# Order of the relu sums, halved GpSimd scaling and the weight of a batch's last values in a fused attention and channel-MLP kernel

## The chip, the cores and the metric

The kernel runs on one core of one Trainium2 chip. The metric is the device time of one execution in microseconds (us). It is given as the median of several executions.

Engine names are short: PE multiplies matrices (PEld is its weight load, which runs beside it), DVE is VectorE, ACT is ScalarE, POOL is GpSimd, and SP issues most DMAs.

## What is computed

For 8 batches of 12 heads, 448 rows and a head width of 64, attention runs on root-mean-square normalised q and k. Its output, laid out as `x` with 768 columns, then goes through a low-rank mix along the rows and a channel MLP with a hidden width of 3072:

```
q_n, k_n = rmsnorm(q, g_q), rmsnorm(k, g_k)
attn = softmax(q_n @ k_n.T / 8);  x = attn @ v          # 8 x 448 x 768
h = x.T @ U @ V                                         # rank 32, along the rows
u = x + h.T
out = u + relu(u @ w_ch1) @ w_ch2                       # 768 -> 3072 -> 768
```

## The kernel before

**Attention.** Work goes by pairs of heads: pair p holds two heads of batch p // 6, so a batch has six pairs. For a pair, squares (`squares`, on ACT for the later pairs) are summed on DVE (`reduce`, L233), ACT turns the sums into factors (`rsqrt`, L238 and L239), and `scale` (L244) multiplies q and k by them. From pair 12 on, `scale` is one GpSimd instruction over 112 x 1024 elements, and SP transposes its result by DMA (`dma_transposes`, L277). `scores` (L295) makes the four 112-column blocks of the scores. Every third block goes into two single banks of PSUM (named `sh` in the profile, drawn from the four-bank pool `mm`), and the others go into a pool of their own (`sc`). ACT takes the exponentials (`expo`, L303). `values` then multiplies by v into a bank of `mm` (`products`, L310), and DVE divides by the row sums and writes `x` (`normalize`, L325 to L338). Its last instruction, L338, is the last reader of that bank.

**MLP.** Tiles of 128 rows are taken two at a time (`mlp_pair`, twelve of them). In its first half, 24 hidden blocks are computed two by two: 12 matmuls (L523) fill a bank `ph`, and a relu (L527; the instruction is L420 on ACT or L422 on DVE) empties it into four quarters of `hT`, called A11, A21, A12 and A22. The second half is Strassen's product in Winograd's form: seven products of 12 matmuls (L511) instead of eight. It needs three sums of relu's output, S1 = A21 + A22, S2 = S1 - A11 and S3 = A11 - A21 (L532 to L534), which DVE makes for four blocks at a time, and a fourth, S4 = A12 - S2 (L556), in three instructions after the third product. S3 is written over A21 and S4 over A12. All of them read two bf16 operands from SBUF. In the first such pair, `combine` (L507) also still makes sums of the weights. The product banks, like `ph`, `o` and `sh`, come from the four-bank pool `mm`.

**What sets the order.** The program is emitted by hand into in-order queues, one for each engine. The MLP is a generator that yields after every step (6 or 12 matmuls). Each yield hands control back to `weave` (L678), which has a list of attention pieces with weights and spreads them over a stretch of the MLP: before each piece it takes MLP steps (`step`, L672) until the piece's share of the columns is done. In `attention`, the last two pieces of a batch are its pair 5's two `values` (L666, L667), with weight 1 each. The sums of relu's output are emitted inside the MLP step that also emits the relu, so they stand on DVE ahead of whatever attention piece follows that step. After batch 7, a plain loop runs the rest of the MLP (L913).

Of the kernel before, what the change touches and what calls it, by code (L numbers as in the profile page):

```python
# [14 lines left out]
OP = AluOpType  # L15
# [3 lines left out]
def kernel(  # L19
# [13 lines left out]
    nc = tc.nc  # L33
    B, H, S, D = q.shape
# [6 lines left out]
    NJ = 4  # L41
    SP = S // NJ
# [72 lines left out]
    def rs_of(p, n=1, of=None):  # L115

        c = 16 * (p % 6)
        return (of or (banks0[3][0:SP] if p < 8 else rms))[:, c:c + 16 * n]
# [122 lines left out]
    def scale(p):  # L241
        t, a = divmod(p, 2)
        qkns[p] = norm.tile([SP, NJ, 4, D], BF16, tag="qkn", name="qkn", bufs=2)
        (nc.gpsimd if p >= 12 else nc.vector).tensor_tensor(  # L244
            qkns[p].rearrange("p j g d -> p g j d"),
            qk_of[t][0:SP, a].rearrange("p s h (j d) -> p (s h) j d", d=D),
            rs_of(p).rearrange("p (g j) -> p g j ()", j=NJ).to_broadcast([SP, 4, NJ, D]),
            OP.mult)

    def k_side(p):  # L250

# [250 lines left out]
    S3, S4 = A21, A12  # L502
# [6 lines left out]
    def product(bank, left, right, start, cols=slice(0, HALF)):  # L509
        for k in range(KH // 2):  # L510
            nc.tensor.matmul(bank, left[:, k, :], right[:, k, cols], start=start and k == 0,  # L511
                             stop=k == KH // 2 - 1, skip_group_check=not start)
            if k == 5:
                yield cols.stop - cols.start

    def mlp_pair(g):
        t0, u, last = 2 * g + 2, u_of(2 * g + 2, 2), 2 * g + 4 == 28
        for k in range(KH // 2):
            ph = ps_mm.tile([P, 4, P], FP32, tag="mm", name="ph")
            for j in range(2):  # L520
                hc, out = 2 * k + j, ph[:, 2 * j:2 * j + 2].rearrange("p a n -> p (a n)")
                for dc in range(KD):
                    nc.tensor.matmul(out, w1b[:, dc, hc * P:(hc + 1) * P], u[:, dc, :],  # L523
                                     start=(dc == 0), stop=(dc == KD - 1))
                if j == 0:
                    yield 2 * P
            relu(hB[:, 0:4, k, :], ph, k % 3)  # L527
            if g == 1 and k in (1, 4, 7, 9):
                combine(12 + (1, 4, 7, 9).index(k))
            if k % 4 == 3:  # L530
                ks = slice(k - 3, k + 1)
                nc.vector.tensor_tensor(S1[:, ks], A21[:, ks], A22[:, ks], OP.add)  # L532
                nc.vector.tensor_tensor(S2[:, ks], S1[:, ks], A11[:, ks], OP.subtract)  # L533
                nc.vector.tensor_tensor(S3[:, ks], A11[:, ks], A21[:, ks], OP.subtract)  # L534
            yield 2 * P
        have_read([t0, t0 + 1])
        x0, x1 = x_of(t0), x_of(t0 + 1)
        c0, c1 = slice(0, HALF), slice(HALF, dm)
        osb0, osb1 = new_osb(), new_osb()

        def bank():
            return ps_mm.tile([P, HALF], FP32, tag="mm", name="po")

        W = bank()
        yield from product(W, A11, B11, True)
        nc.scalar.copy(part, W)
        yield HALF
        Z = bank()
        yield from product(Z, A22, T4, True)
        nc.vector.tensor_tensor(osb1[:, c0], Z, x1[:, c0], OP.add)  # L550
        yield HALF
        yield from product(W, A12, B21, False)
        nc.vector.tensor_tensor(osb0[:, c0], W, x0[:, c0], OP.add)
        for k in range(0, KH // 2, 4):
            ks = slice(k, k + 4)
            nc.vector.tensor_tensor(S4[:, ks], A12[:, ks], S2[:, ks], OP.subtract)  # L556
        if last:
            put(t0, osb0, c0)
        yield HALF
        X = bank()  # L560
        yield from product(X, S2, T2, True)
        nc.vector.tensor_tensor(osb0[:, c1], X, part, OP.add)  # L562
        nc.gpsimd.tensor_tensor(osb0[:, c1], osb0[:, c1], x0[:, c1], OP.add)  # L563
        yield HALF
        parts = [slice(0, HALF // 2), slice(HALF // 2, HALF)] if last else [slice(0, HALF)]
        Ys = [bank() for _ in parts]
        for Y, c in zip(Ys, parts):
            d = slice(HALF + c.start, HALF + c.stop)
            yield from product(Y[:, c], S1, T1, True, c)
            nc.vector.tensor_tensor(osb1[:, d], Y[:, c], x1[:, d], OP.add)  # L570
            yield c.stop - c.start
        yield from product(X, S3, T3, False)
        nc.vector.tensor_tensor(part, X, part, OP.add)  # L573
        both = osb1.rearrange("p (h n) -> p h n", h=2)
        nc.gpsimd.tensor_tensor(both, both, part.rearrange("p n -> p () n").to_broadcast([P, 2, HALF]), OP.add)  # L575
        put(t0 + 1, osb1)
        yield HALF
        for Y, c in zip(Ys, parts):
            d = slice(HALF + c.start, HALF + c.stop)
            yield from product(Y[:, c], S4, B22, False, c)  # L580
            nc.vector.tensor_tensor(osb0[:, d], Y[:, c], osb0[:, d], OP.add)
            if last:
                put(t0, osb0, d, (nc.sync, nc.scalar))
            yield c.stop - c.start
        if not last:
            put(t0, osb0)

    def attention(b):
        items = []

        def add(weight, fn, *args):
            items.append((weight, lambda: fn(*args)))

        starts = (0, 3, 6, 8, 11, 14, 16, 19, 22) if b == 1 else range(0, 24, 3)
        ends = dict(zip(starts, [*starts[1:], 24]))
        apart.update((6 * b + i // 4, i % 4) for i, e in ends.items() if e - i == 3)

        def run(p, kc):
            i = 4 * (p - 6 * b) + kc
            if i in ends:  # L600
                add(3 if i == 3 else 2 if b == 1 and i % 8 == 0 or b == 2 and i == 0 else 1, session, i)
            add(0 if i in ends else 1, expo, p, kc)

        def session(i):
            for j in range(i, ends[i]):
                scores(6 * b + j // 4, (j % 4,))

        for p in range(b * 6, b * 6 + 6):
            t, odd = divmod(p, 2)
            early = p < 12  # L610
            if p == 12:
                add(0, gains, p)
            run(p, 0)
            if p == 11:
                add(0, touch, 7)
                add(0, load, 7)
                add(0, load_v, 7)
            elif p >= 13 and p + 3 < NP:
                add(0, reduce, p + 3)
            elif early and odd:  # L620
                add(0, rsqrt, p + 1, 2)
                add(0, scale, p + 1)
            elif early and p > 6:
                add(0, scale, p + 1)
            run(p, 1)
            if not odd and p >= 14 and p + 2 < NP:
                add(0, rsqrt, p + 2, 2)
            if p >= 12 and p + 2 < NP:
                add(0, scale, p + 2)
                add(0, dma_transposes, p + 2)  # L630
            if p % 6:
                add(1, values, p - 1, 0)
            if p == 11:
                add(0, reduce, 12)
            if early and not odd:
                add(0.5, transposes, p + 1)
                if p < 10:
                    add(0, reduce, p + 2)
            if p + 1 < NP and p > 11:
                add(0, gains, p + 1)  # L640
            run(p, 2)
            if p % 6:
                add(1, values, p - 1, 1)
            if early and not odd:
                if p < 10:
                    add(0, reduce, p + 3)
                for a in range(2):
                    if p != 8:
                        add(0, squares, (10 if p == 6 else 12) + a)
            if p >= 12 and t + 2 < NT:  # L650
                add(0, squares, p + 4, "act")
            if odd and p > 11:
                if t + 3 < NT:
                    add(0, load, t + 3)
                if t + 2 < NT:
                    add(0, load_v, t + 2)
            if not odd and t + 1 < NT:
                add(0, cast_v, t + 1)
            run(p, 3)
            if early and odd and p < 11:  # L660
                add(1, transposes, p + 1)
            if p == 9:
                add(0, touch, 6)
                add(0, load, 6)
                add(0, load_v, 6)
        add(1, values, b * 6 + 5, 0)  # L666
        add(1, values, b * 6 + 5, 1)  # L667
        return items

    at = [0.0]  # L670

    def step(fill):  # L672
        n = next(fill, None)
        if n is not None:
            at[0] += n
        return n
# [170 lines left out]
    with tc.manual_schedule():  # L847
# [62 lines left out]
        for b, key in ends.items():  # L910
            weave(fill, place(key, 0.05), attention(b))
            weave(fill, place(key, 0.6), mixing(b))
        for _ in fill:  # L913
            pass


# [28 lines left out]
```

## Time and profile before

| what | value |
|---|---|
| median of 3 runs | 573.9 us (572.37 to 574.25) |
| profiled execution, its own time | 574.8 us |
| its span in the profile | 572.9 us |
| PE busy | 557.1 us, 97% |
| DVE busy | 349.2 us, 61% |
| ACT busy | 305.1 us, 53% |
| POOL busy | 169.5 us, 30% |
| mean share of the TensorE clock granted | 0.997 |

The span runs from the first to the last recorded instruction, and the execution's own time is 1.9 us longer. A row of the waits view reads: engine and line that waited, then the engine and line that ended the wait, then us in total, number of waits and the longest. A row of the timeline reads: start, duration, engine, line, operation, output and input tiles, shapes, count, and in brackets the idle time before it with what ended it. Waits of PE are counted from the modelled end of the matmul before, those of PEld from the end of the last weight load.

### The profile page before, as it was taken

To read this page: it belongs to the slowest core of one execution; us is meant where nothing else is said; L and a number is where in the kernel's file an instruction comes from. 1 tells how busy PE (TensorE), PEld (TensorE's weight loads), DVE (VectorE), ACT (ScalarE), POOL (GpSimd) and SP (SyncE) were. 2 spreads that over 40 slices of the span, in tenths; PEclk is the share of its full clock that TensorE was granted. 3 is DMA by queue.
4 is the path that set the end of the run, shared out by engine and by line. 5 is a ranking of instruction groups with operands and counts; after the bars stand their busy time and mean duration, and the time that the engine had idled before them with its cause. 6 is when DMAs were issued, how large, how long until landed. Compare 5 with 4: busy or idle time off the path is not lost.

```text
span 572.9 us, 13177 instructions
## 1 busy us (share of the span) xinstructions
PE 557.1 (97%) x5468; PEld 389.2 (68%) x5469; DVE 349.2 (61%) x766; ACT 305.1 (53%) x515; POOL 169.5 (30%) x139
## 2 busy tenths in 40 slices
PE   7999999999999999989999999999999999999996
PEld 3665665767677587676785775776867758777784
DVE  5967867687655655665566678376565554643332
ACT  6966540779267563586547770765716745202020
POOL 5956025343052230531313430432304320010101
PEclk9999999999999999998999999999999999999999
DMA  8999996955373561554447564635606101040101
GB/s 272 279 243 237 204 264 167 203 146 160 99 129 115 137 156 43 123 148 128 94 132 157 138 159 89 148 85 154 163 15 135 31 17 57 9 103 2 56 1 56
DMA packets 108284, 72.39 MB, mean 126 GB/s; under 512 B 56656, under 2 KB 104768, under 8 KB 108224
## 3 DMA queue, kind: packets, MB, share of 16 engines
q1 hardware_dynamic: 96704, 61.70, 42.3%
q0 software_dynamic: 11008, 9.44, 10.2%
q8 instruction: 43, 0.70, 0.5%
q10 hardware_dynamic: 512, 0.41, 0.2%
q14 instruction: 17, 0.14, 0.1%
HBM read 56.78 MB, written 11.01 MB: 118 GB/s over the span
## 4 chain that ended last, share of the span: by engine, by line
PE 80%; DVE 9%; DMA 4%; ACT 2%; POOL 1%; issue 1%; SPq 1%; POOLq 0%; DVEq 0%; ACTq 0%
PE ph L523 32%; PE po L511 25%; PE o L310 6%; PE sc L295 4%; PE ph L448 3%; PE po L466 3%; PE sh L295 3%; DMA qkT<-qkn 2%; DVE hT L534 2%; DVE xr L389 1%; DMA hT<-in_q_dram 1%; DVE hT L532 1%; ACT hT L420 1%; DVE hT L533 1%; DVE comb L507 1%
## 5 line engine op out<-in xcount | busy, mean ns | idle before, releaser
L523 PE MATMUL ph<-ur,w1b 128*128 128x256 bf16 x1728 | 204.2, 274 | 1.3 <-DVE xr L338 1.3
L523 PEld LDWEIGHTS <-w1b 128*128 128x128 bf16 x1728 | 164.9, 98 | 32.0 <-issue 9.6
L511 PEld LDWEIGHTS <-hT 128*128 128x128 bf16 x1032 | 96.3, 98 | 66.4 <-issue 9.7
L420 ACT ACTIVATE hT<-ph 128x512 bf16<-128x512 f32 (+1 forms) x112 | 65.9, 589 | 110.7 <-PE ph L523 103.3
L303 ACT ACTIVATE E<-sc 112x896 bf16<-112x896 f32 x138 | 123.1, 918 | 2.4 <-PE sc L295 2.3
L244 POOL TENSOR_TENSOR qkn<-qk,rms 112x1024 bf16<-112x1024 f32 x36 | 70.5, 1959 | 124.1 <-ACT rms L239 99.0
L511 PE MATMUL po<-w2b,hT 128*128 128x384 bf16 (+1 forms) x588 | 104.4, 323 | 0.2 <-ACT hT L420 0.2
L303 ACT ACTIVATE E<-sh 112x448 bf16<-112x448 f32 x108 | 53.4, 543 | 90.3 <-PE sh L295 90.3
L511 PE MATMUL po<-comb,hT 128*128 128x384 bf16 (+1 forms) x444 | 78.8, 322 | 0.4
L422 DVE TENSOR_SCALAR hT<-ph 128x512 bf16<-128x512 f32 (+1 forms) x58 | 38.6, 666 | 51.3 <-PE ph L523 47.7
L563 POOL TENSOR_TENSOR osb<-osb,xr 128x384 f32<-128x384 f32 x12 | 11.0, 913 | 191.4 <-DVE osb L562 185.4
L310 PEld LDWEIGHTS <-E 112*128 112x128 bf16 x1536 | 61.1, 98 | 9.3 <-issue 1.6
L310 PE MATMUL o<-va,E 112*128 112x65 bf16 x1344 | 57.2, 194 | 0.6 <-ACT E L303 0.5
L532 DVE TENSOR_TENSOR hT<-hT 128x512 bf16<-128x512 bf16 x36 | 21.0, 583 | 34.8 <-ACT hT L420 33.6
L233 DVE TENSOR_REDUCE sums<-sq 112x16 f32<-112x1024 f32 x32 | 38.7, 1210 | 3.8 <-ACT sq L228 3.8
L295 PE MATMUL sc<-qkT 64*128 64x448 bf16 x268 | 39.9, 351 | 0.7 <-ACT qkT L282 0.3
L325 DVE RECIPROCAL rec<-o 128x4 f32<-128x4 f32 x84 | 15.0, 178 | 40.3 <-PE o L310 39.7
L466 PE MATMUL po<-w2b,hT 128*128 128x384 bf16 x192 | 35.2, 326 | 0.1
L295 PEld LDWEIGHTS <-qkT 64*128 64x128 bf16 x376 | 14.9, 94 | 28.9 <-issue 14.6
L228 ACT ACTIVATE sq<-qk 112x1024 f32<-112x1024 f32 x32 | 33.7, 1054 | 0.0
L334 DVE TENSOR_TENSOR xr<-o,rec 128x192 bf16<-128x192 f32 (+1 forms) x108 | 31.5, 310 | 2.9
L575 POOL TENSOR_TENSOR osb<-osb,part 128x768 f32<-128x768 f32 x12 | 21.8, 1813 | 37.1 <-DVE part L573 37.1
(123 smaller groups left out, 520.5 us busy)
## 6 DMA issues: line engine op xcount, KB each, us to landing
qk<-in_q_dram SPq DMA_DIRECT2D x44, 256.0 KB, 4.2
qk<-in_k_dram SPq DMA_DIRECT2D x44, 256.0 KB, 4.8
vt<-in_v_dram SPq DMA_DIRECT2D x17, 512.0 KB, 5.9
w1b<-in_moe_w_ch_dram POOLq DMA_DIRECT2D x6, 768.0 KB, 21.6
w2b<-in_moe_w_ch_dram POOLq DMA_DIRECT2D x6, 768.0 KB, 34.0
out_dram<-osb SPq DMA_DIRECT2D x8, 336.0 KB, 3.0
comb<-in_v_dram SPq DMA_DIRECT2D x5, 512.0 KB, 8.7
out_dram<-osb SPq DMA_DIRECT2D x7, 288.0 KB, 3.0
```

The source lines that it names most:

```text
L228: nc.scalar.activation(dst, src, AF.Square)
L233: nc.vector.tensor_reduce(rs_of(p, of=sums).rearrange("p (s h j) -> p s h j", s=2, h=2)[:, :, hs], sqs[p].rearrange("p (s h j d) -> p s h ...
L244: (nc.gpsimd if p >= 12 else nc.vector).tensor_tensor(qkns[p].rearrange("p j g d -> p g j d"), qk_of[t][0:SP, a].rearrange("p s h (j d) -> ...
L295: nc.tensor.matmul(sc[hh][0:n, 0:S], flat[pp, c:c + n], blocks(p)[pp, :, 0], start=True, stop=True)
L303: nc.scalar.activation(dst, src, AF.Exp, scale=float(D) ** 0.5)
L310: nc.tensor.matmul(o[:, i, :], E[:, hh, c:c + P], va[:, hl, kc, :], start=(kc == 0), stop=(kc == NJ - 1))
L334: nc.vector.tensor_tensor(xr[:, k:k + n, d0:d0 + D], o[:, i:i + n, 0:D], rec[:, i:i + n].rearrange("p c -> p c ()").to_broadcast([P, n, D] ...
L420: nc.scalar.activation(out, ph, AF.Relu)
L422: nc.vector.tensor_relu(out, ph)
L466: nc.tensor.matmul(po, left(hc), w2b[:, half, hc, :], start=(hc == 0), stop=(hc == KH - 1))
L511: nc.tensor.matmul(bank, left[:, k, :], right[:, k, cols], start=start and k == 0, stop=k == KH // 2 - 1, skip_group_check=not start)
L523: nc.tensor.matmul(out, w1b[:, dc, hc * P:(hc + 1) * P], u[:, dc, :], start=(dc == 0), stop=(dc == KD - 1))
```

## The change

It has four edits:

1. `scale` on GpSimd (pairs 12 to 47) is issued as two instructions of 112 x 512 elements, one for q's half of the heads and one for k's, in place of one of 112 x 1024. For the pairs scaled on DVE nothing is different.
2. The sums S1, S2, S3 and S4 of every MLP pair, and four of the `combine` sums, are not emitted where they stood. They are put in a list `pending`, and each call of `step` first emits the oldest one of the list, then the MLP step. So at most one sum precedes each MLP step, and the attention pieces that `weave` puts between the step with the relu and the next one come ahead of it.
3. The first of a batch's last two `values` gets weight 2 in place of 1, so that one more share of the MLP stands between it and the piece before it.
4. The last loop calls `step`, so that it too empties the list.

```diff
@@ scale @@
-        (nc.gpsimd if p >= 12 else nc.vector).tensor_tensor(
-            qkns[p].rearrange("p j g d -> p g j d"),
-            qk_of[t][0:SP, a].rearrange("p s h (j d) -> p (s h) j d", d=D),
-            rs_of(p).rearrange("p (g j) -> p g j ()", j=NJ).to_broadcast([SP, 4, NJ, D]),
-            OP.mult)
+        out = qkns[p].rearrange("p j g d -> p g j d")
+        x = qk_of[t][0:SP, a].rearrange("p s h (j d) -> p (s h) j d", d=D)
+        rs = rs_of(p).rearrange("p (g j) -> p g j ()", j=NJ)
+        for g in (slice(0, 2), slice(2, 4)) if p >= 12 else (slice(0, 4),):
+            (nc.gpsimd if p >= 12 else nc.vector).tensor_tensor(
+                out[:, g], x[:, g], rs[:, g].to_broadcast([SP, g.stop - g.start, NJ, D]), OP.mult)
@@ mlp_pair @@
+    pending = []
+
+    def later(fn, *args):
+        pending.append(lambda: fn(*args))
+
...
-                combine(12 + (1, 4, 7, 9).index(k))
+                later(combine, 12 + (1, 4, 7, 9).index(k))
             if k % 4 == 3:
                 ks = slice(k - 3, k + 1)
-                nc.vector.tensor_tensor(S1[:, ks], A21[:, ks], A22[:, ks], OP.add)
-                nc.vector.tensor_tensor(S2[:, ks], S1[:, ks], A11[:, ks], OP.subtract)
-                nc.vector.tensor_tensor(S3[:, ks], A11[:, ks], A21[:, ks], OP.subtract)
+                later(nc.vector.tensor_tensor, S1[:, ks], A21[:, ks], A22[:, ks], OP.add)
+                later(nc.vector.tensor_tensor, S2[:, ks], S1[:, ks], A11[:, ks], OP.subtract)
+                later(nc.vector.tensor_tensor, S3[:, ks], A11[:, ks], A21[:, ks], OP.subtract)
...
-            nc.vector.tensor_tensor(S4[:, ks], A12[:, ks], S2[:, ks], OP.subtract)
+            later(nc.vector.tensor_tensor, S4[:, ks], A12[:, ks], S2[:, ks], OP.subtract)
@@ attention @@
-        add(1, values, b * 6 + 5, 0)
+        add(2, values, b * 6 + 5, 0)
         add(1, values, b * 6 + 5, 1)
@@ step @@
     def step(fill):
+        if pending:
+            pending.pop(0)()
         n = next(fill, None)
...
-        for _ in fill:
+        while step(fill) is not None:
             pass
```

## The prediction

> **What bounds the kernel now.** I read the page first, then the waits, then the timeline around the longest wait, then one table of stages and a few rows of durations.
>
> ```profile
> PE 557.1 (97%) x5468; PEld 389.2 (68%) x5469; DVE 349.2 (61%) x766; ACT 305.1 (53%) x515; POOL 169.5 (30%) x139
> PE 80%; DVE 9%; DMA 4%; ACT 2%; POOL 1%; issue 1%; SPq 1%; POOLq 0%; DVEq 0%; ACTq 0%
> ```
>
> PE is the bound: it is idle for only 572.9 - 557.1 = 15.8 us. About 5 us of that is the tail after the last matmul, some 3.5 us more is in the first 40 us (PE is busy for 16.74 and 19.73 us of the first two 20 us), and neither is touched by the change. What can be won is therefore single microseconds: PE's gaps between about 120 and 500 us. The chain puts 9% on DVE, about 50 us, but most of that ran while PE multiplied; it is no measure of a gain. The waits name the gaps.
>
> ```profile
> DVE hT L532 <- ACT hT L420: 33.6, 22, 3.2
> ...
> PEld L295 <- DVE xr L338: 4.8, 7, 1.9
> ...
> PE sh L295 <- DVE xr L338: 3.5, 6, 1.6
> ...
> PEld L523 <- DVE xr L338: 2.0, 2, 1.1
> ...
> PE ph L523 <- DVE xr L338: 1.3, 2, 0.6
> ...
> PE o L310 <- ACT E L303: 0.5, 1, 0.5
> ```
>
> The largest waits of PE on an engine end at L338, the last reader of an `o` bank: PE wants a bank of `mm` and normalize has not emptied it. Why it is late is seen in the timeline of the longest such wait:
>
> ```profile
> 253.56 0.47 DVE L532 TENSOR_TENSOR hT<-hT 128x512 bf16<-128x512 bf16 x1 [1.16 <-ACT hT L420]
> 253.70 1.23 POOL L214 CAST va<-vt 112x1024 bf16<-112x1024 f32 x1
> ...
> 254.07 1.14 DVE L533 TENSOR_TENSOR hT<-hT 128x512 bf16<-128x512 bf16 x1
> ...
> 254.90 2.07 POOL L244 TENSOR_TENSOR qkn<-qk,rms 112x1024 bf16<-112x1024 f32 x1
> 255.13 2.12 DVE L534 TENSOR_TENSOR hT<-hT 128x512 bf16<-128x512 bf16 x1
> ...
> 257.17 0.17 DVE L325 RECIPROCAL rec<-o 128x4 f32<-128x4 f32 x1
> ...
> 257.91 0.36 PE L295 MATMUL sh<-qkT 64*128 64x448 bf16 x1 [1.59 <-DVE xr L338]
> ```
>
> A sum that starts under a running GpSimd instruction lasts until just after that one ends: L534 from 255.13 to 257.25, L244 to 256.97. Alone it takes 0.42 us. So three sums of 1.2 us become 3.7 us, they stand ahead of normalize, and PE stands for 1.59 us. The rows of durations say the same (min/median/max in ns):
>
> ```profile
> L534 DVE TENSOR_TENSOR hT<-hT x36: 415/418/2123, 132.3 to 555.7; 128x512 bf16<-128x512 bf16 x36
> L244 POOL TENSOR_TENSOR qkn<-qk,rms x36: 1898/1905/2409, 92.5 to 456.8; 112x1024 bf16<-112x1024 f32 x36
> ```
>
> The same picture (sums stretched to 1.1 to 2.1 us, then a late normalize) stands before the waits near 188, 307, 332, 386 and 460 us. Near 125 us it is `combine` that is stretched. The wait near 257 us has a second cost. The table of stages has length, busy times of PE, PEld, DVE, ACT and POOL, and the granted clock:
>
> ```profile
> 255.30:258.70 3.40, 1.81 (x14) 0.82 (x13) 3.37 (x6) 2.10 (x4) 1.67 (x1) 1.00 0.40 77
> 258.70:262.10 3.40, 3.40 (x18) 2.41 (x17) 0.88 (x1) 1.79 (x4) 0.00 (x0) 0.50 0.92 236
> ```
>
> After the one stretch in which PE was busy for only 1.81 of 3.40 us, the clock is 0.50 for 3.40 us, and half of those, 1.7 us, is lost.
>
> **The change part by part.**
>
> *Sums one per step, behind the attention pieces* (edit 2). It removes no instruction. Where three sums stood ahead of a normalize, there is now none, or one or two that were left from steps before. It acts on the nine waits for L338. PE's rows give 3.5 + 1.3 = 4.8 us; PEld's give 4.8 + 2.0 = 6.8 us. At 257 us the two `sh` matmuls start 1.94 us apart (255.97 and 257.91), though elsewhere in the trace the two start together; PEld's 1.85 is the nearer to that, so I take 6.8 us, with 4.8 as the other end. With the 1.59 us stand gone the halved clock should go: 1.7 us, or nothing if other gaps fall into one such stretch.
>
> The sums also leave a blocking place: L532 stood 33.6 us in 22 waits for ACT's relu, with normalize queued behind it. A step later that relu is mostly done. What is late next: S2 is read by the fourth product, S4 by the last. The last S1, S2, S3 are out by the third step after the last relu, and the fourth product starts with the seventh; a step of 6 matmuls takes 0.98 us (chain rows "PE po L511 x6"), so three steps or more, 3 us, cover a sum of 0.42 to 2.1 us. The S4 sums have as many. I cost these new waits at nothing; without that cover they are a rival below.
>
> *GpSimd scaling in halves* (edit 1). It adds 36 instructions. A blocked sum now waits at most for one half, about 1905 / 2 = 0.95 us, in place of 1.9. That DVE does get in between two GpSimd instructions is in the trace: at 183.28 us a sum waits out one L244, runs, and the cast issued after it lasts 1.24 in place of 1.04 us. The fixed cost of a GpSimd instruction has two bounds. L575 takes 1813 ns for twice the elements of L563 at 913 ns: 2 x 913 - 1813 = 13 ns. L778 takes 402 ns for 128 columns and 834 for 384: 1.69 ns a column, so 186 ns fixed. I take 13 to 186, near the first, as those are of the longer kind. POOL is 30% busy, which hides it, except where the chain runs through a scaling and its transpose (97.89 and 107.52 us, pairs 12 and 13): two times 0.01 to 0.19, I take 0.2 us in all.
>
> Before a sum that meets a half there is a residue: in five of the nine places one sum of about 0.42 us may still stand ahead of a normalize, half of the time under a half. I take 0.3 us each, 1.5 us in all; 0 and 5 x 0.95 = 4.8 are the ends.
>
> *More MLP ahead of the last values* (edit 3). The wait of L310 for an exponential, 0.5 us near 146 us, is at a batch's last values and should go. All earlier pieces of a batch move forward by a few per cent of a stretch, by a step at most. Those are six matmuls each way, covered by a PE queue that is full; I take nothing, with 0.5 us either way per batch as bounds (the longest wait of that kind), some 3 us.
>
> *The last loop* (edit 4) has no attention beside it: nothing.
>
> **The sum.** Against the profiled execution: 574.8 - 6.8 - 1.7 + 1.5 + 0.2 - 0.5 = **567.5 us**. That execution is 0.9 us above the median of 573.9, and the runs spread by 1.9 us, about one halved stretch of clock. From the median it would be 566.6 if that run had it, 568.3 if not; I keep 567.5.
>
> **The Trainium skill, two places.** The trace halves the clock after 1.59 us of standing in 3.4 us. The page "TensorE: Matmul & The Clock Gate", section "Why this matters for your kernels", advises against gaps over some 3 us, which would make this stretch no consequence of the gap: by it the sum would be 569.2. The row above it decides here. And the rows bound a GpSimd instruction's fixed cost by 13 and 186 ns, while the page "GPSIMD Engine Reference", section "3.1 Elementwise — side-by-side cycle accounting", has about 156 ns for DVE's dispatch and two hops in place of one on GpSimd, which speaks against halving; by that, an estimate of 0.3 us a scaling, the two places in the chain would cost 0.6, a sum of 567.9.
>
> **The rivals.**
>
> - *The sums stay in the way.* One per step is still one ahead of each normalize, and each meets a half. For it: the largest stretch of scaling (two L244 and a cast, 5 us) is longer than two steps. Against it: one blocked sum is 1.3 us, not 3.7. Then only half of 6.8 goes, with the clock: 574.8 - 3.4 - 1.7 + 0.2 = 569.9, or 571.6 without the clock. About 571.
> - *The gain is given back.* PE goes faster into ACT, busy 17.19 of the 20 us from 125 to 145. PE's gaps would then end at the exponentials. Against it: over the span ACT is 53% busy and its waits for PE (103.3 us at L420) show slack. Time 573 to 575.
> - *Slower: a product waits for its sum.* S2 or S4 is pushed behind attention work and halves of scaling until the fourth or the last product has to stand. It decides once DVE is more than three steps, 3 us, behind. Price: about 1 us in each of the nine pairs beside attention. With the gain of the first part reduced to 4.8 and the clock lost again: 574.8 - 4.8 + 1.5 + 9 = 580.5; with half the pairs, 576. Against it: the longest stretched run of sums was 3.7 us and DVE is 61% busy.
>
> **How the numbers follow.** Forecast 0.62 (own range 565 to 570), sums in the way 0.15, given back 0.11, slower 0.12. The low end, 564.0, has no residue and also ends 2 us of the smaller waits (L295 for ACT's L282, 1.5; L361 for L338, 0.6). The high end, 573.4, takes in the second case and the edge of the third. What a measurement of this kernel tells from no change is about 0.3%, 1.7 us. Faster by more: 0.62 + 0.15 less a little, 0.76; within: 0.12; slower: 0.12.
>
> **What would show it.** Right: the waits of PE and PEld for L338 fall below 2 us together, no sum lasts over 1.4 us, the clock is 1.00 from 125 to 510 us, and PE's idle falls by some 6 us. Half instructions of L244 near 960 to 1,050 ns. Wrong: waits of L511 for DVE's sums, new waits of L310 for L303, or a stretch of half clock at another place.

## The result and the profile after

The changed kernel takes **566.64 us** (median of 6 runs, 566.12 to 568.81), the kernel before 573.83 us in the same job (6 runs, 572.37 to 576.21). The ratio is 0.988, with a 95% interval from 0.9854 to 0.9907. The forecast was 567.5. The profiled execution of the changed kernel took 566.27 us, with a span of 564.5, against 574.8 and 572.9.

Its page, with busy times and shares of the span first and the chain by engine after it:

```profile
PE 552.0 (98%) x5469; PEld 388.2 (69%) x5469; DVE 339.7 (60%) x766; ACT 303.8 (54%) x515; POOL 179.3 (32%) x175
...
PE 89%; ACT 4%; DVE 2%; DMA 2%; issue 1%; SPq 0%; POOLq 0%
```

PE is idle for 12.5 us in place of 15.8, and the chain's share of DVE falls from 9% to 2%. DVE's busy time falls by 9.5 us though it does the same work: S1 to S4 take 7.9 us less (76.3 to 68.4) and the `combine` sums 2.1 less; other rows are up by some 0.5. That is time in which a sum waited for GpSimd and was counted as busy. The middle of the kernel, in one table of stages (length, then PE, PEld, DVE, ACT and POOL busy, then the clock), once for the kernel before and once for the changed one, each up to its eleventh MLP pair's start:

```profile
125.00:509.00 384.00, 377.82 (x3711) 269.03 (x3712) 235.15 (x534) 215.82 (x357) 100.76 (x66) 1.00 0.44 109
```

```profile
125.00:500.00 375.00, 373.39 (x3714) 268.09 (x3713) 226.92 (x532) 214.54 (x357) 109.87 (x97) 1.00 0.44 112
```

All that was won, 9 us in these two executions, lies here. PE's idle time in the stage falls from 6.2 to 1.6 us. The other 4.4 us are in its busy time. The stretch of half clock is 1.7 of them. Another 1.7 are `sh` matmuls (17.4 to 15.7 us in the stage): two that start together take 0.36 us of PE, and two that start apart 0.36 each. What the rest is stays open. The waits of the changed kernel (L339 is L338 of before, L296 is L295, L304 is L303, L529 is L523):

```profile
PE sc L296 <- ACT E L304: 1.4, 4, 0.4
...
PEld L362 <- DVE hT L520: 1.0, 3, 0.3
...
PEld L296 <- DVE xr L339: 0.6, 2, 0.3
...
PEld L529 <- DVE xr L339: 0.4, 1, 0.4
```

No PE row waits for normalize any more, and PEld's two rows have gone from 6.8 to 1.0 us. Ahead of them stands a wait that was short before (0.3 us, once): scores (`sc`) for an exponential. The rows of durations of the sums (all emitted at L520 now) and of the scaling, min/median/max in ns:

```profile
L520 DVE TENSOR_TENSOR hT<-hT x144: 406/424/1328, 133.2 to 554.1; 128x512 bf16<-128x512 bf16 x144
L248 POOL TENSOR_TENSOR qkn<-qk,rms x72: 1039/1045/3045, 92.7 to 450.3; 112x512 bf16<-112x512 f32 x72
```

The longest sum takes 1.33 us in place of 2.12. A half of the scaling (L248) has a median of 1,045 ns, so two take 185 ns more than the whole one of 1,905. This is the timeline at the place where PE stood for 1.59 us before:

```profile
252.44 1.04 POOL L214 CAST va<-vt 112x1024 bf16<-112x1024 f32 x1
...
252.70 0.18 DVE L326 RECIPROCAL rec<-o 128x4 f32<-128x4 f32 x1 [1.05 <-PE o L311]
252.92 0.36 DVE L335 TENSOR_TENSOR xr<-o,rec 128x192 bf16<-128x192 f32 x1
253.19 0.21 DVE L339 TENSOR_TENSOR xr<-o,rec 64x64 bf16<-64x64 f32 x1
253.32 2.79 DVE L520 TENSOR_TENSOR hT<-hT 128x512 bf16<-128x512 bf16 x3
253.44 2.40 POOL L248 TENSOR_TENSOR qkn<-qk,rms 112x512 bf16<-112x512 f32 x2
...
254.56 0.36 PE L296 MATMUL sh<-qkT 64*128 64x448 bf16 x2
254.76 0.35 PE L296 MATMUL sc<-qkT 64*128 64x448 bf16 x2
255.30 0.98 ACT L304 ACTIVATE E<-sh 112x448 bf16<-112x448 f32 x2
255.47 0.36 PE L296 MATMUL sc<-qkT 64*128 64x448 bf16 x2 [0.35 <-ACT E L304]
```

Normalize now runs ahead of the sums, and the two `sh` matmuls start together. The three sums still take 2.79 us under the scaling, but nothing that PE needs stands behind them. New is the last row: the second pair of `sc` matmuls waits for an exponential to empty its bank.

### The profile page after: what moved, and what is told of

Same layout as the page of the kernel before. It is cut to its first block, busy times and chain, and to the rows that moved or that the text cites. A ratio compares the mean times of both kernels' runs of the same rounds, so it can differ in the third digit from the quotient of the medians.

```text
span 564.5 us, 13202 instructions
## 1 busy us (share of the span) xinstructions
PE 552.0 (98%) x5469; PEld 388.2 (69%) x5469; DVE 339.7 (60%) x766; ACT 303.8 (54%) x515; POOL 179.3 (32%) x175
## 4 chain that ended last, share of the span: by engine, by line
PE 89%; ACT 4%; DVE 2%; DMA 2%; issue 1%; SPq 0%; POOLq 0%
PE ph L529 32%; PE po L512 29%; PE o L311 7%; PE po L467 5%; PE sc L296 4%; PE ph L449 3%; PE sh L296 3%; ACT E L304 2%; PE px L388 1%; ACT hT L421 1%; DMA hT<-in_moe_V_dram 1%; DMA qk<-in_q_dram 1%; PE bank L311 1%; PE sc L710 1%; PE ph L477 1%
## 5 line engine op out<-in xcount | busy, mean ns | idle before, releaser
L529 PE MATMUL ph<-ur,w1b 128*128 128x256 bf16 x1728 | 202.7, 273 | 0.0
L529 PEld LDWEIGHTS <-w1b 128*128 128x128 bf16 x1728 | 164.0, 98 | 29.1 <-issue 9.1
L512 PEld LDWEIGHTS <-hT 128*128 128x128 bf16 x1032 | 96.5, 98 | 65.0 <-issue 7.9
L421 ACT ACTIVATE hT<-ph 128x512 bf16<-128x512 f32 (+1 forms) x112 | 65.5, 587 | 116.1 <-PE ph L529 108.6
L304 ACT ACTIVATE E<-sc 112x896 bf16<-112x896 f32 x138 | 123.1, 918 | 2.3 <-PE sc L296 2.3
L248 POOL TENSOR_TENSOR qkn<-qk,rms 112x512 bf16<-112x512 f32 x72 | 80.4, 1138 | 111.2 <-ACT rms L239 86.5
L512 PE MATMUL po<-w2b,hT 128*128 128x384 bf16 (+1 forms) x588 | 103.6, 323 | 0.2 <-ACT hT L421 0.2
L304 ACT ACTIVATE E<-sh 112x448 bf16<-112x448 f32 x108 | 52.9, 543 | 78.6 <-PE sh L296 78.6
L520 DVE TENSOR_TENSOR hT<-hT 128x512 bf16<-128x512 bf16 x144 | 68.4, 492 | 21.3 <-ACT hT L421 19.0
L512 PE MATMUL po<-comb,hT 128*128 128x384 bf16 (+1 forms) x444 | 78.3, 322 | 0.0
L569 POOL TENSOR_TENSOR osb<-osb,xr 128x384 f32<-128x384 f32 x12 | 12.9, 1072 | 189.1 <-DVE osb L568 168.1
L296 PE MATMUL sc<-qkT 64*128 64x448 bf16 x268 | 39.7, 351 | 1.8 <-ACT E L304 1.1
L390 DVE TENSOR_TENSOR xr<-px,xr 128x384 bf16<-128x384 f32 x56 | 29.5, 550 | 5.9 <-PE px L386 3.2
```

The lines of the kernel that those rows point to most:

```text
L248: (nc.gpsimd if p >= 12 else nc.vector).tensor_tensor(out[:, g], x[:, g], rs[:, g].to_broadcast([SP, g.stop - g.start, NJ, D]), OP.mult)
L296: nc.tensor.matmul(sc[hh][0:n, 0:S], flat[pp, c:c + n], blocks(p)[pp, :, 0], start=True, stop=True)
L304: nc.scalar.activation(dst, src, AF.Exp, scale=float(D) ** 0.5)
L421: nc.scalar.activation(out, ph, AF.Relu)
L520: pending.append(lambda: fn(*args))
```

## The experiments

**Theories.** *Place*, the prediction's: the sums cost because they stand ahead of normalize, so edit 2 brings nearly everything and edit 1 nothing. *Stretch*: they cost because each waits out a GpSimd instruction, so edit 1 brings about as much. *Shift*: the new weight moved attention pieces away from sums, or towards something worse. The edits were made one by one, two by two, and then varied. Where a median of the kernel before is named, it is that of the same job: 573.64 us for the first four kernels, 574.05 for the next four, 574.5 for the last four.

**The sums alone** (edits 2 and 4).

```diff
-                nc.vector.tensor_tensor(S1[:, ks], A21[:, ks], A22[:, ks], OP.add)
+                later(nc.vector.tensor_tensor, S1[:, ks], A21[:, ks], A22[:, ks], OP.add)
...
     def step(fill):
+        if pending:
+            pending.pop(0)()
```

> The sums one per step alone: GpSimd scaling whole, weight 1. If the place of the sums is the cause, most of the 7.2 us goes: about 568 us, and the waits of PE and PEld for normalize's last instruction fall from 11.6 us to under 3. If the length of the GpSimd instruction is the cause, single sums are still stretched to 2.1 us ahead of a normalize and little goes: about 572.

568.09 us, ratio 0.9905 (0.9887 to 0.9924). Its waits for normalize (L528 is L523 of before):

```profile
PEld L295 <- DVE xr L338: 2.1, 6, 0.4
...
PEld L528 <- DVE xr L338: 1.1, 1, 1.1
...
PE ph L528 <- DVE xr L338: 0.6, 1, 0.6
...
PE sh L295 <- DVE xr L338: 0.2, 1, 0.2
```

From 11.6 us for PE and PEld together to 4.0, where under 3 were expected, and 5.6 us of time. The longest sum still takes 2,119 ns in this kernel. The place where PE stood for 1.59 us shows why (L519 are the sums):

```profile
254.38 0.18 DVE L325 RECIPROCAL rec<-o 128x4 f32<-128x4 f32 x1
...
255.00 2.52 DVE L519 TENSOR_TENSOR hT<-hT 128x512 bf16<-128x512 bf16 x2
255.16 2.08 POOL L244 TENSOR_TENSOR qkn<-qk,rms 112x1024 bf16<-112x1024 f32 x1
...
256.24 0.36 PE L295 MATMUL sh<-qkT 64*128 64x448 bf16 x2
```

Two sums are still stretched, but normalize ran ahead of them, and the `sh` matmuls start together. So the place by itself takes away more than half of the gain; that stretched sums cost nothing elsewhere does not follow, since halves beside this edit bring some 3.5 us more (below). The longest wait left (1.1 us) is the one near 125 us, behind a `combine` that the edit does not touch.

**The halves alone** (edit 1).

```diff
...
+        for g in (slice(0, 2), slice(2, 4)) if p >= 12 else (slice(0, 4),):
+            (nc.gpsimd if p >= 12 else nc.vector).tensor_tensor(
+                out[:, g], x[:, g], rs[:, g].to_broadcast([SP, g.stop - g.start, NJ, D]), OP.mult)
```

> The GpSimd scaling in halves alone, sums in blocks of three where they were. If the length of the GpSimd instruction is the cause: each sum waits for at most one half (1.05 us in the trace after the change), the block takes 2.5 to 3 in place of 3.7 us, and about half of the gain is here, 570 us. If the place is the cause: 572 to 573.8, the waits for normalize stay over 7 us together.

567.71 us, ratio 0.9906 (0.9885 to 0.9926): 5.9 us, as much as the sums alone, though the sums stand where they stood. The timeline at the place near 184 to 189 us, where before PE stood for two `sh` matmuls in turn (0.38 and 0.41 us of idle; L533 to L535 are S1 to S3 here):

```profile
182.59 1.22 POOL L248 TENSOR_TENSOR qkn<-qk,rms 112x512 bf16<-112x512 f32 x1
182.95 1.15 DVE L534 TENSOR_TENSOR hT<-hT 128x512 bf16<-128x512 bf16 x1
183.77 1.23 POOL L214 CAST va<-vt 112x1024 bf16<-112x1024 f32 x1
184.02 1.25 DVE L535 TENSOR_TENSOR hT<-hT 128x512 bf16<-128x512 bf16 x1
...
185.20 0.17 DVE L326 RECIPROCAL rec<-o 128x4 f32<-128x4 f32 x1
...
187.42 0.36 PE L296 MATMUL sh<-qkT 64*128 64x448 bf16 x2
```

Each sum waits out one GpSimd instruction and no more, so the last one (S3) lasts 1.25 us in place of 2.12, normalize starts that much sooner, and the `sh` matmuls start together. The waits of PE and PEld for normalize fall from 11.6 to 3.6 us, much as with the sums alone, and one stand of 0.9 us is left. The stretch theory holds as well as the other: each edit by itself takes away two thirds of these waits, from two ends. The gain is above what either theory expected of this kernel (570 us, or 572 and more).

**The weight alone** (edit 3).

```diff
-        add(1, values, b * 6 + 5, 0)
+        add(2, values, b * 6 + 5, 0)
```

> The weight of a batch's last values alone. Both theories give nothing much: 573.3, with the 0.5 us wait of the products for an exponential gone and the waits for normalize as before. A third, that the shift of the attention pieces moved the normalizes away from the sums, gives 570 or less.

574.29 us (12 runs), ratio 1.0016 (0.9999 to 1.0032): nothing that can be told from no change, and no gain. The products' wait of 0.5 us for an exponential is gone from PE's rows, as expected, but they wait for normalize there instead (1.2 us, once).

**Scaling cut short.** The order of before, with GpSimd's instruction on a quarter of the elements; the kernel leaves out the other three quarters of the scaling. The instruction's median is 613 ns, in place of 1,905.

```diff
...
+        g = slice(0, 1) if p >= 12 else slice(0, 4)
...
-            qkns[p].rearrange("p j g d -> p g j d"),
+            qkns[p].rearrange("p j g d -> p g j d")[:, g],
...
```

> The order of before, but from pair 12 on GpSimd scales only the first of four slices, about 0.5 us in place of 1.9; the other three are left out and keep the values of pairs 10 and 11, so the attention of those pairs is not the reference's. If the stretch by GpSimd is what makes the block of sums long enough to hurt, the block takes 1.2 to 2 us and nearly all of the waits for normalize go: 567 to 568.5. If three sums in a row are enough by themselves, the waits stay over 6 us together: 571 to 573.

567.18 us, ratio 0.9888 (0.9866 to 0.991). The longest first sum of a block takes 1,217 ns in place of 1,843 and the longest third one 834 in place of 2,123, and no `sh` matmul has a wait for normalize in PE's rows; PEld's rows for it come to 1.6 us, the longest 0.4. Three sums in a row ahead of normalize are thus harmless if GpSimd hardly holds them up. It takes both to make the stand: the place and the stretch. (The shorter scaling also lets q and k be ready sooner; PEld's waits of scores for them fall by 0.8 us, so that is a small part at most of the 6.5.)

**Both, without the weight** (edits 1, 2 and 4).

> Sums one per step and halves, weight 1. If the two edits cure the same waits: 566 to 567, 1 us under either alone. If each cures waits of its own, 573.6 - 5.5 - 5.9 = 562 to 563. If the weight costs the 0.6 us that its single run showed, this is at or below the whole change, 566.

565.02 us, ratio 0.9844 (0.982 to 0.9868), 1.6 us below the whole change's 566.64. 9.0 us is less than 5.6 + 5.9 = 11.5, so the two edits share part of the waits, and each has some of its own. The waits of PE and PEld for normalize show the same: 11.6 us before, 4.0 and 3.6 with one edit, 1.4 with both.

**The sums and the weight** (without the halves).

> Sums one per step and the weight, scaling whole. If the weight does nothing: as the sums alone, 568. If it matters for where single sums land: 566.5.

567.76 us, ratio 0.9904 (0.988 to 0.9929), as the sums alone: with whole scaling the weight does nothing that the time shows. In PE's rows it moves waits: the 0.6 us of MLP matmuls (`ph`) and the products' 0.5 are gone, and scores wait longer for ACT (1.4 us in four for an exponential, 1.0 in two for a relu, against 0.7 and 0.3).

**The halves and the weight** (without the sums).

> Halves and the weight, sums in blocks. If the weight does nothing: as the halves alone, 567.7. If it moves normalizes into the blocks as in its single run: 568.3.

573.73 us (12 runs), ratio 0.9995 (0.9976 to 1.0014): the whole gain of the halves is gone. The shift theory allowed for something worse; no expectation had this size. The timeline near 256 us shows it:

```profile
253.63 1.04 POOL L214 CAST va<-vt 112x1024 bf16<-112x1024 f32 x1
...
254.01 0.94 DVE L533 TENSOR_TENSOR hT<-hT 128x512 bf16<-128x512 bf16 x1 [1.16 <-ACT hT L421]
254.63 2.40 POOL L248 TENSOR_TENSOR qkn<-qk,rms 112x512 bf16<-112x512 f32 x2
254.99 1.15 DVE L534 TENSOR_TENSOR hT<-hT 128x512 bf16<-128x512 bf16 x1
...
256.06 1.26 DVE L535 TENSOR_TENSOR hT<-hT 128x512 bf16<-128x512 bf16 x1
257.24 0.17 DVE L326 RECIPROCAL rec<-o 128x4 f32<-128x4 f32 x1
...
257.98 0.36 PE L296 MATMUL sh<-qkT 64*128 64x448 bf16 x1 [1.86 <-DVE xr L339]
```

Each of the three sums meets a GpSimd instruction of its own (cast, half, half), the block lasts 3.3 us, and PE stands for 1.86 us, longer than before the change. Halves shorten one sum's wait; they do not help a block that meets as many instructions as it has sums. Which it meets is set by where the attention pieces fall, and the weight moves them. One other loss is near 136 us, where a pair of `sc` matmuls stands 0.85 us for ACT's scaling of q by the gains (L282 of before). That a small shift of the pieces cost 6 us in the medians is shown, its split by places only for these two. Some 2 us of it go with the clock: among runs with a granted clock of 0.998 or more, this kernel takes 571.1 and 571.4 us and the halves alone 567.0 to 567.7, but ten of its twelve runs have 0.992 to 0.996.

**All sums of the list at one step** (the whole change, but `step` empties the list).

```diff
-        if pending:
+        while pending:
```

> The whole change, but a step empties the whole list, so three sums stand in a row again, only behind the attention pieces that follow the relu. If it is the place behind the attention's work that helps, as the whole change: 566.6. If it is the spreading, one per step, that helps: back to the halves with the weight, 568.

570.14 us, ratio 0.9934 (0.991 to 0.9958): 3.5 us above the whole change, and 3.6 below the halves with the weight, where the block stood where it was. Neither expectation holds: moving the block behind an attention piece brings about half of the difference, and spreading it the other half. Its new waits have the mixing's L390 in them (`PE po L512 <- DVE xr L390`, 0.9 us in 3 waits): much less of normalize is behind the block (its waits in PE's rows are 0.5 us, against 2.4 in the halves with the weight), but other work is.

**The whole change again, and again without the weight**, on one chip.

> The whole change once more, beside the next kernel on one chip. If the weight of 2 costs time: 566.5, 1 to 2 us above the next one.

> Sums one per step and halves with weight 1, once more. If the weight costs what the separate calls showed: 565.0, below the whole change by 1 to 2 us, with two waits fewer of the scores for an exponential. If the two calls differed by chance, both are within 0.5 us.

566.54 us, ratio 0.9866 (0.9845 to 0.9887), and 564.29 us, ratio 0.9829 (0.9807 to 0.9851). The weight costs 2.2 us here, after 1.6 in the first measurement. The two intervals just overlap, but among runs with a granted clock of 0.998 or more the kernels stand apart both times: 565.9 to 566.7 us with the weight, 563.7 to 565.0 without. The version without it is the fastest of all that were run. Of the waits of scores for an exponential, 1.4 us in four with the weight (both runs of the whole change have them), the version without it has 0.3 us in one here and 0.7 in two in its first run. A second wait of scores grows with the weight, that of `sh` for a bank which ACT's relu has not emptied (`PE sh L296 <- ACT hT L421`): 1.0 us in two, against 0.3 in one. The products' wait for an exponential, 0.5 us without the weight, is gone with it. These rows come to 0.9 to 1.3 us; the rest of the 1.6 and 2.2 is not traced. At 248 us the changed kernel, first, has its second `sc` pair waiting; without the weight (its first run, second) all four start together, one step later:

```profile
247.73 0.36 PE L296 MATMUL sc<-qkT 64*128 64x448 bf16 x2
248.37 0.61 ACT L421 ACTIVATE hT<-ph 128x512 bf16<-128x512 f32 x1
248.54 0.36 PE L296 MATMUL sc<-qkT 64*128 64x448 bf16 x2 [0.44 <-ACT E L304]
```

```profile
248.33 0.36 PE L296 MATMUL sh<-qkT 64*128 64x448 bf16 x2
248.53 0.57 PE L296 MATMUL sc<-qkT 64*128 64x448 bf16 x4
```

The last values' extra share moves the earlier pieces forward, scores among them, and the two `sc` banks are then still waiting for ACT.

**Quarters** (both edits, weight 1, four GpSimd instructions).

```diff
-        for g in (slice(0, 2), slice(2, 4)) if p >= 12 else (slice(0, 4),):
+        for g in [slice(i, i + 1) for i in range(4)] if p >= 12 else (slice(0, 4),):
```

> Sums one per step, weight 1, scaling in four instructions. If a blocked sum's wait for one GpSimd instruction still costs: that wait falls from 1.05 to about 0.6 us (0.86 of it work, split in two, and 0.185 fixed) and the time to 564. If nothing of it is on the path any more, the time stays at 565, with GpSimd busier by 72 x 0.185 = 13 us.

566.06 us, ratio 0.9849 (0.9831 to 0.9866), against 0.9829 with halves: the intervals overlap, and there is no further gain. A quarter has a median of 612 ns, so four take 543 ns more than the whole one, 181 for each instruction added, and GpSimd is busy for 13.6 us more than with halves, near the 13 expected. Of its waits, those of scores for a transposed q and k (`PEld L296 <- ACT qkT L283`) come to 1.6 us in 3, against 0.8 in 2 with halves; that the longer scaling makes them is argued, not shown.

**Less weight** (both edits, 0.3 in place of 1).

```diff
-        add(1, values, b * 6 + 5, 0)
+        add(0.3, values, b * 6 + 5, 0)
```

> Sums one per step, halves, and weight 0.3 for the first of the last values, in place of 1. If what the weight does is to push a batch's scores towards the exponentials, less weight spreads them and helps a little more: 564.5. If the weight merely shuffles which piece meets which sum, the time can go either way: 565 to 567, and the waits are at other places.

571.81 us, ratio 0.9943 (0.9925 to 0.9961), 7.5 us slower than with weight 1, outside what either guess allowed. (Its one run with a clock of 0.998 or more takes 569.77, 5.5 to 6.0 more than such runs with weight 1.) Its waits:

```profile
PEld L311 <- ACT E L304: 5.6, 5, 1.5
PE o L311 <- ACT E L304: 5.0, 5, 1.4
```

With too little MLP ahead of the last values, the products stand for the batch's last exponential, five times, up to 1.4 us. So edit 3 has a real wait to cure; at weight 1 it is 0.5 us at one batch in PE's rows, and at 2 the cure costs more in scores.

## Why the prediction was right, and where its steps were not

The time and the sign were right: 567.5 forecast, 566.64 measured, and all six runs lie within 1.4 us of the forecast. The steps behind it were only partly so, and their errors balanced: that the forecast came within 1 us is partly luck. Leaving out its 0.5 us for the third edit, the prediction's sum gives 568.0 us for the other edits; they took 565.0 and 564.3. So the sums and the halves were forecast 3 to 4 us too weak, and the weight, forecast as a gain of 0.5, cost 1.6 to 2.2.

- **Bound and place: right.** The gain lies in PE's waits for normalize between 125 and 510 us. They were put at 6.8 us by PEld's rows, and PEld's rows fell by 5.8. Taking PEld's row rather than PE's 4.8 fits the stage: PE's idle time fell by 4.6 us there, and `sh` pairs that no longer start apart saved 1.7 of busy time.
- **"GpSimd scaling in halves": wrong as a term.** It was costed at +0.2 us, as a mere limit on the residue of edit 2. Alone it brings 5.9 us (567.71), and beside the sums some 3.5 more (5.6 to 9.0, each against the kernel before in its own job). The timeline that the prediction shows had it: of the block's 3.7 us, 2.5 were waits for GpSimd, and the cut-short scaling confirms that with most of them gone no stand at `sh` is left. The working gave the whole wait to one of two causes that were both necessary.
- **The fixed cost of a GpSimd instruction** was bounded by 13 and 186 ns and taken near 13; it is 2 x 1,045 - 1,905 = 185 ns. The row of the smaller instructions (L778) was the right one. POOL's idle time hid it, as forecast: POOL is busy 9.8 us longer (36 x 0.185 = 6.7 of it are fixed cost) and the time did not rise.
- **"Sums one per step", 6.8 us less a residue of 1.5:** alone 5.6 us. That is near the forecast's net 5.3, clock left out; but the 1.5 counted on halves.
- **"More MLP ahead of the last values": wrong in sign.** Forecast: 0.5 us won, nothing lost, with 0.5 us per batch as bounds. Measured: 1.6 and 2.2 us lost beside the other two edits, 6 lost beside the halves alone. The wait of products for the exponential did fall (0.5 us to none in PE's rows), but scores moved into the exponentials and relus on ACT: 1.4 us in four, and 1.0 in two. The prediction had that mechanism in its rival "the gain is given back", but not as a cost of this edit.
- **The clock, 1.7 us: mis-sized.** It was taken as a consequence of the 1.59 us stand that would go with it. Of the 17 runs of the kernel before beside the first four experiments, 8 have a granted clock of 0.998 or more and take 571.7 to 572.9 us; 9 have 0.997 or less and take 573.6 to 574.9. The changed kernel has both kinds too: 0.998 or 0.999 at 566.1 to 566.7, 0.995 at 568.2 and 568.8. So the 1.7 us are there in some runs and not in others, before and after. Among runs with a clock of 0.998 or more the gain is about 6 us, from some 572.4 to 566.4. Whether the change makes such stretches rarer is open: 14 of the 45 runs of the kernel before beside the experiments have 0.998 or more, and 6 of the ten runs of the changed kernel.
- **The residue** was right in kind: 0.3 and 0.4 us are the longest waits left, 1.0 us together for PEld against 1.5.
- **The signs:** the waits for normalize under 2 us, no sum over 1.4 us, halves of 1,045 ns and a clock of 1.00 in the stage came true. PE's idle time fell by 3.3 us over the span, not by some 6, since much of the gain lay in its busy time.
- **The products that wait for a sum** did not come: S2 and S4 were early enough. In the changed kernel the only such row is PEld's for the mixing (L362), 1.0 us in three waits; without the weight there is also one of 0.4 us for a product (L512).

Of the rivals, "the sums stay in the way" fits no kernel with one sum per step, but sums in the way are what the halves with the weight kept (573.73).

## What to carry to other kernels

When a wait needs two things at once (here a block of sums ahead of normalize, and a GpSimd instruction that holds each sum), either one's removal shows more than half of the gain (5.6 and 5.9 of 9.0 us): price each edit against the kernel with the other left out, not as shares of one sum. A small shift in an interleaving by weights is not free even when it moves work by a single step; look for the next wait on both sides of it, here 0.3 and 2 were both worse than 1. And an edit that comes with a good one should be tried without it: the change gained 7.2 and 8.0 us, and without its third edit 9.0 and 10.2.

## What the runs showed of the hardware

- A DVE sum with two bf16 operands in SBUF, which takes 0.42 us alone, lasts until some 0.28 us after the end of the GpSimd instruction that was running when it started, and then runs ahead of GpSimd's next one (with the halves alone, a cast behind such a sum lasts 1.23 us in place of 1.04). With whole scaling its longest is 2.12 us, with halves 1.33. The page "SBUF — State Buffer" of the Trainium skill, section "SBUF: two separate sides", describes such a pair of ports shared by the two engines and held for a whole instruction; these rows agree.
- A half-clock stretch does not follow from a stretch of low PE use by itself. Before the change, 3.40 us with PE busy for 1.81 were followed by a clock of 0.50. In the kernel with the halves and the weight the same stand, longer, was not (length, then PE and the other engines busy, then the clock):

```profile
254.30:257.70 3.40, 1.82 (x15) 1.22 (x13) 3.33 (x5) 2.46 (x4) 2.73 (x3) 1.00 0.35 68
257.70:261.10 3.40, 3.12 (x38) 2.46 (x39) 2.04 (x4) 1.63 (x3) 0.00 (x0) 1.00 0.69 151
```

- Several profiles (the first one without the weight among them) have their half-clock stretch at about 8 us instead, in the head, where PE is fed by the first loads; there the first hidden block of the MLP starts 1.5 to 2.1 us later than in the profile before:

```profile
8.06:11.47 3.41, 2.76 (x13) 1.38 (x13) 1.77 (x3) 2.57 (x7) 1.11 (x1) 0.50 1.09 379
```

What decides between the two is not settled by these runs.
